# Per-tile shift of the row maxima, one two-bank output tile for a pair of score tiles, and a fourth pair turned by TensorE

## The chip, the cores and the metric

The kernel runs on one core of one Trainium2 chip. The metric is the device time of one execution in microseconds (us). Beside it stands one execution recorded by the hardware profiler; the trace's times count from that execution's first instruction.

## The reference

Three stages follow each other. Attention has a bias that a small network makes from positions; its output, with the heads side by side, passes a Fourier mixing with a two-layer network, and then a gated network.

```python
scores = scale * np.matmul(q, k.transpose(0, 1, 3, 2))      # B, H, S, D = 4, 8, 576, 64
...
scores = scores + bias.transpose(2, 0, 1)[None, :, :, :]
scores = scores - np.max(scores, axis=-1, keepdims=True)
attn = np.exp(scores)
attn = attn / (np.sum(attn, axis=-1, keepdims=True) + 1e-09)
attn_out = np.matmul(attn, v)
...
X = np.fft.fft(np.fft.fft(x, axis=1), axis=2)               # x: (4, 576, 512), heads side by side
u = x + np.real(X)
...
```

The change touches the attention stage and the way from it into the Fourier stage.

## The kernel before, in words

**Tiles.** A head pair `n` is two heads of one batch; there are 16. Each pair of head pairs gives 18 score tiles of 128 rows by 576 keys: eight of the first pair (row tiles 0 to 3, two heads), two of row tile 4 (the last 64 rows, both heads on 128 partitions, one tile for each head pair), eight of the second. They are worked two at a time: a *tile pair* `d`, 72 in all. `c = d % 9` is its place in a group of nine: places 0 to 3 are the row tiles of the first head pair, 4 the two half tiles, 5 to 8 the second head pair.

**The loop.** `attention_phase` is written for engines that run their instructions in the order of the code. One round of its loop (L572) issues work for several tile pairs, with the lags of `LAGS`:

- `scores(d)`: TensorE (PE), 12 matmuls into two PSUM tiles `sc`, of which there are three, two banks each
- `total(u)` (L413): VectorE (DVE), one custom instruction for a tile that adds the bias and takes the row maximum, which a second short instruction writes to `mm`
- `shift(d)` (L433): DVE, one TENSOR_SCALAR on two numbers a partition, minus the maxima plus a constant
- `soft(d-1)`: ScalarE (ACT), one exponential for each tile, with the shifted maximum as its bias
- turning the tile, so that keys lie on partitions. Odd `d` go by PE (`by_pe`, L445): `flip` (L475) transposes into a `sc` tile and ACT copies it to 16 bits (L484), `flip_low` (L489, DVE) makes the remainder and so frees the `sc` tile. Even `d` go by DMA: ACT copies to 16 bits (`high`), GpSimd (POOL) makes the remainder (`low`, L459), and SyncE's queue (SP) issues a DMA transpose (`turn`, L472). `FLIPS = 3` sends the last three pairs by PE whatever their number; so pair 68 is the last that the DMA turns
- `back(u)` (L493): PE, the products with `v` of the pair six rounds earlier, into a PSUM tile `po` of one bank; there are two such tiles, one for each tile of a pair
- `finish(u)` (L513): DVE, when `po` is complete (places 3, 4 and 8): row sums to factors `ri` (L523, L527), then `po` times `ri` into `x` (L531, or L541 for the half tiles). For the two tiles of a pair the steps alternate
- `store(u)` (L545): SP, `x` to a DRAM tensor `xd`

POOL also prepares the next head pair's inputs (L385 to L393).

**The end of the stage.** After round 71 the loop runs on to drain. In each round `after(d - nd)` runs `first_folds` (L779): at -3 SP loads `xd` of batch 0, at 0 the tile pool `ff` is opened on the memory of the closed pools `qk` and `sh` (which held `hl`, the source of the DMA transposes), POOL loads a sine table into it, and SP loads batches 1 and 2; at 3 batch 3. From round 1 of the drain on, two steps a round of `Folds.prep` (L728) run on DVE and ACT for batch 0. Then `fft_phase` begins on PE (L823).

**Rows of the text below.** `s` and `mm` are written by L421, `mm` by L435; `pt` is a turned tile; `lowa`, `lowb` and `raw` are large buffers (bias, inputs, later the loaded `xd`).

Of the kernel before, what the change touches and what calls it, by code (L numbers as in the profile page):

```python
# [9 lines left out]
F32 = mybir.dt.float32  # L10
# [5 lines left out]
ALU = mybir.AluOpType  # L16
PSUM = bass.MemoryType.PSUM

B, H, S, D = 4, 8, 576, 64
# [3 lines left out]
PSC = 2.0**14  # L23
PSH = 14 * math.log(2.0)
# [26 lines left out]
QW = S + 64  # L51
RAW = 2 * (S + 2 * QW)
LAGS = 1, 2, 3, 3, 3, 6
FLIPS = 3
SB = 4
PB = 4
HLB = 3
# [3 lines left out]
def pool(tc, **kw):  # L61

    return tc.tile_pool(reuse_waits="tile", **kw)
# [281 lines left out]
def attention_phase(tc, nc, io, vs, bias, biasl, raw, xd, ident, last, after, es, right):  # L345
# [7 lines left out]
    rq, st, live, pts, outs, xs, hls, mms, Ps = {}, {}, {}, {}, {}, {}, {}, {}, {}  # L353
    pairs = [(b, p) for b in range(B) for p in range(NP)]
    units = []
# [3 lines left out]
    nu = len(units)  # L359
# [53 lines left out]
    def total(u):  # L413
        n, t, h = units[u]
        sc = live.pop(u)
        bv = bias[t // 2][:, t % 2, 2 * pairs[n][1] + h] if t < 4 else biasl[:, pairs[n][1]]
        s = sp.tile([128, S], F32, tag="s", name="s", bufs=SB)
        if u % 2 == 0:
            mms[u // 2] = wp.tile([128, 2, 2], F32, tag="mm", name="mm", bufs=4)
        mm = mms[u // 2]  # L420
        nc.vector.tensor_tensor_reduce(  # L421
            out=s.rearrange("p (x e) -> p x e", x=2),
            in0=sc[:, :, 0:288],
            in1=bv.rearrange("p (x e) -> p x e", x=2),
            scale=0.125,
            scalar=-3.0e38,
            op0=ALU.add,
            op1=ALU.max,
            accum_out=mm[:, 0, u % 2 : u % 2 + 1],
        )  # L430
        live[u] = s

    def shift(d):  # L433
        mm = mms[d]
        nc.vector.tensor_scalar(out=mm[:, 1], in0=mm[:, 0], scalar1=-1.0, scalar2=PSH, op0=ALU.mult, op1=ALU.add)  # L435

    def soft(d):
        P = Pt[d % PB]
        mm = mms.pop(d)
        for x in range(2):  # L440
            s = live.pop(2 * d + x)
            nc.scalar.activation(out=P[:, x, 0:S], in_=s, func=AF.Exp, bias=mm[:, 1, x : x + 1], scale=1.0)  # L442
        Ps[d] = P

    def by_pe(d):  # L445

        return d % 2 == 1 or d >= nd - FLIPS

# [26 lines left out]
    def flip(u):  # L475
        d, x = divmod(u, 2)
        if x == 0:
            room(d)
        P = Ps[d][:, x]
        t = ps_s.tile([128, 2, 512], F32, tag="sc", name="turn").rearrange("p x e -> p (x e)")[:, 0:640]  # L480
# [12 lines left out]
    def back(u):  # L493
        n, t, h = units[u]
        vp = st[n]["v"]
        pt = pts.pop(u)
        if t in (0, 4):
            outs[n, t // 4, h] = ps_o.tile([128, 4, 128], F32, tag="po", name="po")
        po = outs[n, t // 4, h]
        for a in range(1 if t < 4 else 2):  # L500
            hh = h if t < 4 else a
            c = slice(0, 128) if t < 4 else slice(64 * a, 64 * a + 64)
            seq = []
            for j in range(5):
                seq += [(j, j, 0, 65), (j, j, 65, 64)]
            seq += [(5 + j, j, 0, 65) for j in range(5 if by_pe(u // 2) else 4)]
            for i, (x, j, f, w) in enumerate(seq):
                nc.tensor.matmul(  # L508
                    out=po[c, t % 4, 0:w], lhsT=pt[:, x, c], rhs=vp[:, j, hh, f : f + w],
                    start=(i == 0), stop=(i == len(seq) - 1),  # L510
                )

    def finish(u):  # L513
        n, t, h = units[u]
        if t < 3:
            return
        if n not in xs:
            xs[n] = xp.tile([128, 5, 128], F32, tag="x", name="x") if n + 1 < len(pairs) else last
        x = xs[n]
        po = outs.pop((n, t // 4, h))  # L520
        w = 4 if t == 3 else 1
        ri = wp.tile([128, 4], F32, tag="ri", name="ri", bufs=4)
        nc.vector.tensor_scalar(  # L523
            out=ri[:, 0:w], in0=po[:, 0:w, 64], scalar1=PSC * 1e-9, scalar2=vs[:, 0:1], op0=ALU.add, op1=ALU.mult
        )
        yield
        nc.vector.reciprocal(out=ri[:, 0:w], in_=ri[:, 0:w])  # L527
        yield
        if t < 4:
            f = 64 * h if 2 * pairs[n][1] >= H // 2 else 64 - 64 * h  # L530
            nc.vector.tensor_tensor(  # L531
                out=x[:, 0:4, f : f + 64],
                in0=po[:, :, 0:64],
                in1=ri.rearrange("p (w o) -> p w o", o=1).to_broadcast([128, 4, 64]),
                op=ALU.mult,
            )
        else:
            for a in range(2):
                f = 64 * a if 2 * pairs[n][1] >= H // 2 else 64 - 64 * a
                r = slice(64 * a, 64 * a + 64)  # L540
                nc.vector.tensor_scalar(  # L541
                    out=x[0:64, 4, f : f + 64], in0=po[r, 0, 0:64], scalar1=ri[r, 0:1], scalar2=None, op0=ALU.mult
                )

    def store(u):  # L545
        n, t, h = units[u]
        if (t, h) != ((3, 1) if n % 2 else (4, 0)) or n + 1 == len(pairs):
            return
        b, p = pairs[n]
        p = p if 2 * p >= H // 2 else H // 4 - 1 - p  # L550
        f = slice(128 * p, 128 * p + 128)
        x = xs.pop(n)
        nc.sync.dma_start(out=xd[b][0:512, f].rearrange("(t p) d -> p t d", p=128), in_=x[:, 0:4])
        nc.sync.dma_start(out=xd[b][512:S, f], in_=x[0:64, 4])

    yield [lambda n=n, nm=nm: load(n, nm) for n in range(2) for nm in "kqv"]
    yield from prep(0)
# [1 line left out]
    wp = es.enter_context(pool(tc, name="att", bufs=3))  # L559
    sp = e1.enter_context(pool(tc, name="sh", bufs=3, side="right"))  # L560
    xp = es.enter_context(pool(tc, name="xs", bufs=2))
    ps_s = es.enter_context(pool(tc, name="ps_s", bufs=3, space=PSUM))
    ps_o = es.enter_context(pool(tc, name="ps_o", bufs=2, space=PSUM))
    Pt = [wp.tile([128, 2, QW], F32, name=f"P{x}", bufs=1) for x in range(PB)]
    for P in Pt:
        nc.gpsimd.memset(P[:, :, S:QW], 0.0)
# [1 line left out]
    L1, L2, L3, L4, L6, L5 = LAGS  # L568
    nd = nu // 2
    flips = [2 * d + x for d in range(nd) if by_pe(d) for x in range(2)]  # L570
    lows = []
    for d in range(nd + L5 + 2):  # L572
        us = (2 * d, 2 * d + 1) if d < nd else ()
        bs = (2 * (d - L5), 2 * (d - L5) + 1) if 0 <= d - L5 < nd else ()
        fin = [finish(u) for u in bs]

        def step():
            for f in fin:
                next(f, None)

        c = d % 9
        n = 2 * (d // 9) + (c >= 5)
        if us and c in (0, 5) and n + 1 < len(pairs):
            nxt = prep(n + 1)

        for x in lows:
            flip_low(*x)
        lows = []
        if 0 <= d - L1 < nd:
            soft(d - L1)  # L590
        if us:
            scores(d)
        for x in range(2):
            if x == 0 or not us:
                if flips and flips[0] // 2 <= d - L6:
                    lows.append(flip(flips.pop(0)))
            if bs:
                back(bs[x])
        if 0 <= d - L2 < nd:
            high(d - L2)  # L600
        if us:
            total(us[0])
        if 0 <= d - L3 < nd:
            low(d - L3)
        if 0 <= d - L4 < nd:
            turn(d - L4)
        if us:
            next(nxt, None)
            total(us[1])
            shift(d)  # L610
        step()
        if us:
            next(nxt, None)
        step()
        step()
        if us and n + 2 < len(pairs):
            for nm in {0: "k", 1: "q", 2: "v"}.get(c - 5 * (c >= 5), ""):
                load(n + 2, nm)
        for u in (2 * (d - L5 - 1), 2 * (d - L5 - 1) + 1):
            if 0 <= u < nu:  # L620
                store(u)
        if d == nd:
            e1.close()
        after(d - nd)
# [32 lines left out]
TP = 290  # L657
T2 = 289
F_LOAD = -3
F_PREP = 1  # L660
F_STEPS = 2
F_MAX = 5
# [27 lines left out]
class Folds:  # L690
# [82 lines left out]
    def ahead(self, n):  # L773

        if self.done < n:
            next(self.flow, None)


def first_folds(folds):  # L779

    def after(n):
        if n == F_LOAD:
            folds.load(0)
        if n == 0:
            folds.open()
            for b in range(1, B - 1):
                folds.load(b)

        if n == 3:
            folds.load(B - 1)  # L790
        for _ in range(F_STEPS):
            if n >= F_PREP:
                folds.ahead(F_MAX)

    return after
# [965 lines left out]
```

## Time and profile before

| | us |
|---|---|
| median of 3 runs | 1143.27 |
| lowest, highest | 1139.97, 1145.56 |
| the profiled execution | 1141.91 |
| its span, first to last instruction | 1140.0 |

So 1.9 us of the profiled execution lie outside its span, and it is 1.4 us faster than the median. In the span PE is busy for 1030.9 us (90%), DVE 728.8 (64%), ACT 553.5 (49%), POOL 292.1 (26%). Those are means over stages that differ: up to 127 us the bias is made, attention's loop runs from there to about 370 us, its drain to 406, the Fourier stage begins at 406.7, and from about 500 us on PE works almost without a gap. A time in the trace is read as start and duration; a note in brackets is the engine's idle time just before, with the event that ended it.

### The profile page before, as it was taken

To read this page: it belongs to the slowest core of one execution; us is meant where nothing else is said; L and a number is where in the kernel's file an instruction comes from. 1 tells how busy PE (TensorE), PEld (TensorE's weight loads), DVE (VectorE), ACT (ScalarE), POOL (GpSimd) and SP (SyncE) were. 2 spreads that over 40 slices of the span, in tenths; PEclk is the share of its full clock that TensorE was granted. 3 is DMA by queue.
4 is the path that set the end of the run, shared out by engine and by line. 5 is a ranking of instruction groups with operands and counts; after the bars stand their busy time and mean duration, and the time that the engine had idled before them with its cause. 6 is when DMAs were issued, how large, how long until landed. Compare 5 with 4: busy or idle time off the path is not lost.

```text
span 1140.0 us, 25690 instructions
## 1 busy us (share of the span) xinstructions
PE 1030.9 (90%) x10711; PEld 943.3 (83%) x10711; DVE 728.8 (64%) x1826; ACT 553.5 (49%) x1047; POOL 292.1 (26%) x250
## 2 busy tenths in 40 slices
PE   6999877878878299969999999999999999999998
PEld 4778776767777178658999999999999989898997
DVE  5998899999999387477796523334495165352512
ACT  3888788888888234454452212212254234333322
POOL 2777687877676000000000000000001120101000
PEclk8999899999999699989999999999999999999999
DMA  5542177778776940014451000000133000101011
GB/s 164 175 135 89 34 162 168 162 159 168 161 175 125 140 136 1 19 56 130 120 186 48 1 1 2 1 1 1 57 111 109 1 1 1 38 1 47 1 38 47
DMA packets 116626, 90.40 MB, mean 79 GB/s; under 512 B 85721, under 2 KB 97117, under 8 KB 116253
## 3 DMA queue, kind: packets, MB, share of 16 engines
q1 hardware_dynamic: 113496, 79.88, 28.2%
q10 hardware_dynamic: 2724, 5.90, 1.6%
q0 software_dynamic: 288, 2.97, 1.2%
q8 instruction: 84, 1.38, 0.5%
q14 instruction: 34, 0.27, 0.1%
HBM read 58.95 MB, written 9.14 MB: 60 GB/s over the span
## 4 chain that ended last, share of the span: by engine, by line
PE 65%; DVE 17%; POOL 6%; issue 4%; DMA 4%; ACT 3%; SPq 0%; ACTq 0%; POOLq 0%; DVEq 0%
PE h L1287 18%; PE acc L1323 17%; PE psp L1459 5%; PE pu L1434 4%; PE po L1481 4%; POOL hl L459 3%; PE pv L1382 3%; PE y L823 3%; DMA pt<-hl 2%; PE D L870 2%; DVE pt L491 2%; DVE s L421 2%; PE bps L267 2%; DVE bt L311 2%; PE sc L408 2%
## 5 line engine op out<-in xcount | busy, mean ns | idle before, releaser
L1291 ACT ACTIVATE gh<-h 128x256 fp32r<-128x256 f32 x144 | 55.2, 383 | 249.1 <-PE h L1287 246.8
L1292 DVE SCALAR_TENSOR_TENSOR gl<-h,gh 128x256 fp32r<-128x256 f32 x144 | 60.9, 423 | 175.2 <-ACT gh L1291 174.3
L1287 PE MATMUL h<-uh,wh 128*128 128x256 f32 x576 | 162.9, 283 | 2.2 <-DVE gl L1292 2.0
L1323 PE MATMUL acc<-gh,wh 128*128 128x256 f32 x576 | 163.7, 284 | 0.0
L1287 PE MATMUL h<-uh,wl 128*128 128x256 f32 x576 | 162.0, 281 | 1.1 <-DVE wl L995 1.1
L1323 PE MATMUL acc<-gh,wl 128*128 128x256 f32 x576 | 161.7, 281 | 1.4 <-DVE wl L995 1.4
L1287 PE MATMUL h<-ul,wh 128*128 128x256 f32 x576 | 161.9, 281 | 0.0
L1323 PE MATMUL acc<-gl,wh 128*128 128x256 f32 x576 | 161.4, 280 | 0.0
L1079 POOL MEMSET w<- 64x288 f32 x2 | 0.7, 335 | 491.6 <-ACT wsq L976 491.5
L1287 PEld LDWEIGHTS h<-uh,wh 128*128 128x128 f32 x576 | 109.6, 190 | 3.1 <-DVE gl L1292 2.5
L442 ACT ACTIVATE P<-s,mm 128x576 f32<-128x576 f32 x144 | 103.2, 766 | 17.0 <-DVE mm L435 17.0
L1287 PEld LDWEIGHTS h<-uh,wl 128*128 128x128 f32 x576 | 109.6, 190 | 1.3 <-DVE wl L995 1.3
L1323 PEld LDWEIGHTS acc<-gh,wl 128*128 128x128 f32 x576 | 109.0, 189 | 1.7 <-DVE wl L995 1.6
L1287 PEld LDWEIGHTS h<-ul,wh 128*128 128x128 f32 x576 | 109.3, 190 | 0.1
L1323 PEld LDWEIGHTS acc<-gl,wh 128*128 128x128 f32 x576 | 108.9, 189 | 0.3
L1323 PEld LDWEIGHTS acc<-gh,wh 128*128 128x128 f32 x576 | 108.8, 189 | 0.4
L508 PE MATMUL po<-vp,pt 128*128 128x65 f16 (+3 forms) x2322 | 84.1, 196 | 22.3 <-DMA pt<-hl 21.4
L508 PEld LDWEIGHTS <-pt 128*128 128x128 f16 (+1 forms) x2322 | 80.7, 101 | 25.4 <-DMA pt<-hl 21.8
L482 PE MATMUL turn<-ident,P 128*128 128x128 f32 x370 | 57.0, 286 | 45.9 <-DVE pt L491 45.4
L459 POOL TENSOR_TENSOR hl<-P,hl 128x1024 f16<-128x1024 f32 x70 | 88.6, 1289 | 29.5 <-PE sc L408 13.0
L482 PEld LDWEIGHTS turn<-ident,P 128*128 128x128 f32 x370 | 40.7, 144 | 58.8 <-issue 34.3
L250 ACT ACTIVATE mask<-pre 128x576 f16<-128x576 f32 x96 | 61.1, 652 | 25.8 <-PE pre L247 24.5
(245 smaller groups left out, 2665.8 us busy)
## 6 DMA issues: line engine op xcount, KB each, us to landing
w<-in_w_ch SPq DMA_DIRECT2D x32, 512.0 KB, 3.5
vld<-in_v ACTq DMA_DIRECT2D x16, 320.0 KB, 3.5
raw<-in_q SPq DMA_DIRECT2D x16, 320.0 KB, 4.1
raw<-in_v SPq DMA_DIRECT2D x16, 320.0 KB, 4.0
raw<-in_k SPq DMA_DIRECT2D x16, 288.0 KB, 3.2
w<-in_w_in SPq DMA_DIRECT2D x8, 512.0 KB, 3.5
out<-o SPq DMA_DIRECT2D x16, 256.0 KB, 2.0
xd<-x SPq DMA_DIRECT2D x15, 256.0 KB, 4.1
```

The source lines that it names most:

```text
L250: nc.scalar.activation(out=m.rearrange("p (x e) -> p x e", x=2), in_=p[:, :, 0:288], func=AF.Sigmoid, scale=1e30)
L442: nc.scalar.activation(out=P[:, x, 0:S], in_=s, func=AF.Exp, bias=mm[:, 1, x : x + 1], scale=1.0)
L459: nc.gpsimd.tensor_tensor(out=hl[:, :, o : o + c], in0=P[:, :, j : j + c], in1=hl[:, :, j : j + c], op=ALU.subtract)
L482: nc.tensor.transpose(t[:, 128 * k : 128 * k + 128], P[:, 128 * k : 128 * k + 128], ident)
L508: nc.tensor.matmul(out=po[c, t % 4, 0:w], lhsT=pt[:, x, c], rhs=vp[:, j, hh, f : f + w], start=(i == 0), stop=(i == len(seq) - 1),)
L1287: nc.tensor.matmul(out=h, lhsT=st[:, q], rhs=mv[:, k], start=(n == 0), stop=(n == 11))
L1291: nc.scalar.activation(out=gh, in_=h, func=AF.Relu)
L1292: nc.vector.scalar_tensor_tensor(out=gl, in0=h, scalar=0.0, in1=gh.bitcast(F32), op0=ALU.max, op1=ALU.subtract)
L1323: nc.tensor.matmul(out=acc[x, d // 2][:, d % 2], lhsT=st[:, q], rhs=mv, start=(e == 0 and d % 2 == 0 and n == 0), stop=(e == NF - 1 and d ...
L1434: nc.tensor.matmul(out=p[:, 0:CH], lhsT=st[:, q], rhs=mv[:, kk, e], start=(n == 0), stop=(n == 11))
L1459: nc.tensor.matmul(out=p[:, 0:CH], lhsT=st, rhs=mv, start=(n == 0), stop=(n == len(seq) - 1))
L1481: nc.tensor.matmul(out=p, lhsT=st[:, f, c], rhs=mv, start=(n == 0), stop=(n == 11))
```

## The change

- `shift` works on one tile, one number a partition. It follows each `total`, so there are two a tile pair.
- `back` uses one `po` tile of two banks, a bank for each tile of the pair; the pool has one such tile where it had two of one bank. `finish` runs once a tile pair, on both banks together. For the half tiles it writes all 128 partitions of `x[:, 4, 0:64]` in one instruction a head pair (the last head pair still in two), and `store` sends the two halves as two DMAs in place of one.
- `FLIPS = 4`: pair 68 is turned by PE; the last pair that the DMA turns is 66.
- `X_LOAD = 0, 3, 4`: in the drain, batch 1 is loaded at round 0, batch 2 at round 3 (was 0), batch 3 at round 4 (was 3).

```diff
-FLIPS = 3
+FLIPS = 4
...
-    def shift(d):
-        mm = mms[d]
-        nc.vector.tensor_scalar(out=mm[:, 1], in0=mm[:, 0], scalar1=-1.0, scalar2=PSH, op0=ALU.mult, op1=ALU.add)
+    def shift(u):
+        mm = mms[u // 2]
+        x = slice(u % 2, u % 2 + 1)
+        nc.vector.tensor_scalar(out=mm[:, 1, x], in0=mm[:, 0, x], scalar1=-1.0, scalar2=PSH, op0=ALU.mult, op1=ALU.add)
...
-        if t in (0, 4):
-            outs[n, t // 4, h] = ps_o.tile([128, 4, 128], F32, tag="po", name="po")
-        po = outs[n, t // 4, h]
+        if t in (0, 4) and u % 2 == 0:
+            outs[u // 18, t // 4, n % 2] = ps_o.tile([128, 2, 4, 128], F32, tag="po", name="po")
+        po = outs[u // 18, t // 4, n % 2 if t < 4 else 0][:, u % 2]
...
+        ri = wp.tile([128, 2, 4], F32, tag="ri", name="ri", bufs=4)[:, :, 0:w]
         nc.vector.tensor_scalar(
-            out=ri[:, 0:w], in0=po[:, 0:w, 64], scalar1=PSC * 1e-9, scalar2=vs[:, 0:1], op0=ALU.add, op1=ALU.mult
+            out=ri, in0=po[:, :, 0:w, 64], scalar1=PSC * 1e-9, scalar2=vs[:, 0:1], op0=ALU.add, op1=ALU.mult
         )
         yield
-        nc.vector.reciprocal(out=ri[:, 0:w], in_=ri[:, 0:w])
+        nc.vector.reciprocal(out=ri, in_=ri)
         yield
-        if t < 4:
-            f = 64 * h if 2 * pairs[n][1] >= H // 2 else 64 - 64 * h
+        if c != 4:
+            n = ns[0]
+            x = xs[n][:, 0:4].rearrange("p t (h d) -> p h t d", h=2)
             nc.vector.tensor_tensor(
-                out=x[:, 0:4, f : f + 64],
-                in0=po[:, :, 0:64],
-                in1=ri.rearrange("p (w o) -> p w o", o=1).to_broadcast([128, 4, 64]),
+                out=x if ahead(n) else x[:, ::-1],
+                in0=po[:, :, :, 0:64],
+                in1=ri.rearrange("p h (w o) -> p h w o", o=1).to_broadcast([128, 2, 4, 64]),
                 op=ALU.mult,
             )
-        else:
+            return
+        for j, n in enumerate(ns):
+            x = xs[n]
+            if n + 1 < len(pairs):
+                nc.vector.tensor_scalar(
+                    out=x[:, 4, 0:64], in0=po[:, j, 0, 0:64], scalar1=ri[:, j], scalar2=None, op0=ALU.mult
+                )
+                continue
...
-        nc.sync.dma_start(out=xd[b][512:S, f], in_=x[0:64, 4])
+        for a in range(2):
+            f = 128 * p + (64 * a if ahead(n) else 64 - 64 * a)
+            nc.sync.dma_start(out=xd[b][512:S, f : f + 64], in_=x[64 * a : 64 * a + 64, 4, 0:64])
...
-    ps_o = es.enter_context(pool(tc, name="ps_o", bufs=2, space=PSUM))
+    ps_o = es.enter_context(pool(tc, name="ps_o", bufs=1, space=PSUM))
...
             total(us[0])
+            shift(us[0])
...
             total(us[1])
-            shift(d)
+            shift(us[1])
...
+X_LOAD = 0, 3, 4
...
             folds.open()
-            for b in range(1, B - 1):
-                folds.load(b)
-
-        if n == 3:
-            folds.load(B - 1)
+        if n in X_LOAD:
+            folds.load(1 + X_LOAD.index(n))
```

On DVE, a round in which a place-3 pair is finished and the round after it, in which the half tiles are, stand before the change as follows (`ISA` is the custom instruction of `total` and the one that writes its maximum).

```order
L421 ISA s,mm<-sc,lowa 128x576
L421 ISA mm 128x1
L421 ISA s,mm<-sc,lowa 128x576
L421 ISA mm 128x1
L435 TENSOR_SCALAR mm<-mm 128x2
L523 TENSOR_SCALAR ri<-po,vs 128x4 x2
L527 RECIPROCAL ri<-ri 128x4 x2
L531 TENSOR_TENSOR x<-po,ri 128x4x64 x2
L491 TENSOR_TENSOR pt<-turn,pt 128x640
```

The same round in the changed kernel:

```order
L421 ISA s,mm<-sc,lowa 128x576
L421 ISA mm 128x1
L436 TENSOR_SCALAR mm<-mm 128x1
L421 ISA s,mm<-sc,lowa 128x576
L421 ISA mm 128x1
L436 TENSOR_SCALAR mm<-mm 128x1
L530 TENSOR_SCALAR ri<-po,vs 128x8
L534 RECIPROCAL ri<-ri 128x8
L539 TENSOR_TENSOR x<-po,ri 128x2x4x64
L493 TENSOR_TENSOR pt<-turn,pt 128x640
```

One shift has moved up between the two score tiles, and the six instructions of the finish have become three.

On SP, the last transposes and the loads of `xd` (buffers `raw`, `lowb`) stand before the change as follows.

```order
L472 DMA_TRANSPOSE pt<-hl 128x18x128 x2
L553 DMA xd_76<-x 128x4x128
L554 DMA xd_76<-x 64x128
L725 DMA raw<-xd_73 128x4x512
L726 DMA raw<-xd_73 64x512
L472 DMA_TRANSPOSE pt<-hl 128x18x128
L725 DMA lowb<-xd_74 128x4x512
L726 DMA lowb<-xd_74 64x512
L725 DMA lowb<-xd_75 128x4x512
L726 DMA lowb<-xd_75 64x512
L553 DMA xd_76<-x 128x4x128
L554 DMA xd_76<-x 64x128
```

And in the changed kernel:

```order
L474 DMA_TRANSPOSE pt<-hl 128x18x128 x2
L568 DMA xd_76<-x 128x4x128
L571 DMA xd_76<-x 64x64 x2
L742 DMA raw<-xd_73 128x4x512
L743 DMA raw<-xd_73 64x512
L742 DMA lowb<-xd_74 128x4x512
L743 DMA lowb<-xd_74 64x512
L568 DMA xd_76<-x 128x4x128
L571 DMA xd_76<-x 64x64 x2
L742 DMA lowb<-xd_75 128x4x512
L743 DMA lowb<-xd_75 64x512
```

The single transpose between the loads is gone, and the load of `xd_75` (batch 2) stands behind the last store.

## Rows read from the trace of the kernel before

**Rows 1.** Page, part 2: granted TensorE clock in tenths, 40 slices of 28.5 us.

```profile
PEclk8999899999999699989999999999999999999999
```

**Rows 2.** Pairs 9-62: length, busy (count) of PE, PEld, DVE, ACT, POOL; then L435.

```profile
153.88:341.94 188.06, 150.85 (x2659) 136.32 (x2660) 173.61 (x445) 159.51 (x226) 141.04 (x103) 0.99 0.76 167
...
153.88:341.94 188.06, 33.07 (x54) 0.99 0.76 167
```

**Rows 3.** All L435: duration ns min/median/max; then the timeline around one of them.

```profile
L435 DVE TENSOR_SCALAR mm<-mm x72: 168/310/1864, 128.6 to 369.7; 128x2 f32<-128x2 f32 x72
...
252.06 2.13 POOL L459 TENSOR_TENSOR hl<-P,hl 128x1024 f16<-128x1024 f32 x1
252.25 0.08 DVE L421 DVE_READ_ACCUMULATOR2_ANT mm<- 128x1 f32 x1
252.37 1.85 DVE L435 TENSOR_SCALAR mm<-mm 128x2 f32<-128x2 f32 x1
```

**Rows 4.** VectorE's groups: name, shapes, count | busy us, mean ns | idle before, releaser.

```profile
L491 DVE TENSOR_TENSOR pt<-turn,pt 128x640 f16<-128x640 f32 x74 | 60.3, 818 | 4.7 <-ACT pt L484 3.2
...
L435 DVE TENSOR_SCALAR mm<-mm 128x2 f32<-128x2 f32 x72 | 43.2, 600 | 2.5
...
L531 DVE TENSOR_TENSOR x<-po,ri 128x256 f32<-128x256 f32 x30 | 11.2, 416 | 0.0
```

**Rows 5.** VectorE's waits, the same stretch: us in total, times, longest.

```profile
DVE s L421 <- PE sc L408: 6.3, 18, 1.4
```

**Rows 6.** Timeline, the end of the attention stage.

```profile
370.85 7.03 SPq L472 DMA_TRANSPOSE pt<-hl  x1
...
372.24 0.61 POOL L716 DMA_DIRECT2D sin<-in_c_t  x1 [1.42 <-ACT P L442]
...
377.92 0.58 SPq L725 DMA_DIRECT2D lowb<-xd  x1
...
397.77 0.94 PE L508 MATMUL po<-vp,pt 128*128 128x65 f16 x14 [21.39 <-DMA pt<-hl]
397.85 0.69 DVE L746 TENSOR_TENSOR flo<-raw,fhi 128x512 fp32r<-128x512 f32 x1 [17.30 <-DMA pt<-hl]
...
406.70 0.30 PE L823 MATMUL y<-tt,fhi 128*1 128x290 f32 x1
```

**Rows 7.** DMA issues: KB each, median us from issue to landing.

```profile
sin<-in_c_t POOLq DMA_DIRECT2D x1, 1450.0 KB, 25.1
...
pt<-hl SPq DMA_TRANSPOSE x35, 4.6
```

**Rows 8.** Timeline of a late stage; then L1390's ns min/median/max.

```profile
930.64 1.32 POOL L1403 TENSOR_TENSOR vl<-v,vh 128x512 fp32r<-128x512 f32 x1 [6.21 <-ACT vh L1402]
...
930.75 0.15 DVE L1390 TENSOR_SCALAR ve<-mv 128x1 f32<-128x1 f32 x1
...
931.18 0.80 DVE L930 TENSOR_TENSOR ve<-ve 128x1 f32<-128x1 f32 x1 [0.27 <-ACT ve L928]
...
L1390 DVE TENSOR_SCALAR ve<-mv x18: 153/154/156, 928.2 to 1085.2; 128x1 f32<-128x1 f32 x18
```

**Rows 9.** Timeline of the rounds in which places 3 and 4 are finished.

```profile
281.82 0.34 DVE L523 TENSOR_SCALAR ri<-po,vs 128x4 f32<-128x4 f32 x2
...
282.08 0.29 DVE L527 RECIPROCAL ri<-ri 128x4 f32<-128x4 f32 x2
...
283.94 0.74 PE L482 MATMUL turn<-ident,P 128*128 128x128 f32 x5 [1.61 <-DVE pt L491]
...
284.60 1.68 PE L508 MATMUL po<-vp,pt 128*64 128x65 f16 x56
...
286.32 0.22 DVE L523 TENSOR_SCALAR ri<-po,vs 128x1 f32<-128x1 f32 x1 [0.48 <-PE po L508]
...
286.65 1.18 DVE L541 TENSOR_SCALAR x<-po,ri 64x64 f32<-64x64 f32 x4
```

**Rows 10.** Last half tile's finish to last fold; columns as in rows 2.

```profile
376.05:409.25 33.20, 10.05 (x147) 8.75 (x145) 15.56 (x28) 4.86 (x8) 0.00 (x0) 0.64 1.05 166
```

More of the change, by code (lines that the diff above doesn't have):

```diff
@@ L431, in total @@
         live[u] = s
-    def shift(d):
-        mm = mms[d]
-        nc.vector.tensor_scalar(out=mm[:, 1], in0=mm[:, 0], scalar1=-1.0, scalar2=PSH, op0=ALU.mult, op1=ALU.add)
+    def shift(u):
+        mm = mms[u // 2]
+        x = slice(u % 2, u % 2 + 1)
+        nc.vector.tensor_scalar(out=mm[:, 1, x], in0=mm[:, 0, x], scalar1=-1.0, scalar2=PSH, op0=ALU.mult, op1=ALU.add)
     def soft(d):
+        assert d - PB not in Ps
         P = Pt[d % PB]
@@ L511, in back, with ahead, finish @@
                 )
-    def finish(u):
-        n, t, h = units[u]
-        if t < 3:
-            return
[L517 to L522, printed above, removed]
+    def ahead(n):
+        return 2 * pairs[n][1] >= H // 2
+    def finish(d):
+        c = d % 9
+        if c not in (3, 4, 8):
+            return
+        ns = (2 * (d // 9), 2 * (d // 9) + 1)
+        ns = ns if c == 4 else ns[c // 8 : c // 8 + 1]
+        for n in ns:
+            if n not in xs:
+                xs[n] = xp.tile([128, 5, 128], F32, tag="x", name="x") if n + 1 < len(pairs) else last
+        po = outs.pop((d // 9, int(c == 4), int(c == 8)))
+        w = 1 if c == 4 else 4
+        ri = wp.tile([128, 2, 4], F32, tag="ri", name="ri", bufs=4)[:, :, 0:w]
@@ L538, in finish, with store @@
             for a in range(2):
-                f = 64 * a if 2 * pairs[n][1] >= H // 2 else 64 - 64 * a
+                f = 64 * a if ahead(n) else 64 - 64 * a
                 r = slice(64 * a, 64 * a + 64)
                 nc.vector.tensor_scalar(
-                    out=x[0:64, 4, f : f + 64], in0=po[r, 0, 0:64], scalar1=ri[r, 0:1], scalar2=None, op0=ALU.mult
+                    out=x[0:64, 4, f : f + 64], in0=po[r, j, 0, 0:64], scalar1=ri[r, j], scalar2=None, op0=ALU.mult
                 )
-    def store(u):
-        n, t, h = units[u]
-        if (t, h) != ((3, 1) if n % 2 else (4, 0)) or n + 1 == len(pairs):
+    def store(d):
+        n = 2 * (d // 9) + (d % 9 == 8)
+        if d % 9 not in (4, 8) or n + 1 == len(pairs):
@@ L548, in store @@
             return
         b, p = pairs[n]
-        p = p if 2 * p >= H // 2 else H // 4 - 1 - p
+        p = p if ahead(n) else H // 4 - 1 - p
         f = slice(128 * p, 128 * p + 128)
@@ L574, in attention_phase @@
         bs = (2 * (d - L5), 2 * (d - L5) + 1) if 0 <= d - L5 < nd else ()
-        fin = [finish(u) for u in bs]
+        fin = finish(d - L5) if bs else iter(())
         def step():
-            for f in fin:
-                next(f, None)
+            next(fin, None)
         c = d % 9
@@ L618, in attention_phase @@
                 load(n + 2, nm)
-        for u in (2 * (d - L5 - 1), 2 * (d - L5 - 1) + 1):
-            if 0 <= u < nu:
-                store(u)
+        if 0 <= d - L5 - 1 < nd:
+            store(d - L5 - 1)
         if d == nd:
```

## The prediction

> **What bounds the kernel now.** I read the page's slices first, then the busy times of the attention loop, then single instructions of VectorE, then the end of that stage. The clock row [rows 1] shows one hole behind the start-up: slice 14, about 370 to 399 us, at 0.6. The change works just before and in it.
>
> The loop first. From the first total of pair 9 to that of pair 63 are 54 tile pairs in 188.06 us, 3.48 us each; VectorE is busy for 173.61 of them (92%), ScalarE 159.51 (85%), TensorE 150.85 (80%), GpSimd 141.04 (75%) [rows 2]. So VectorE is the bound, with ScalarE close behind. In that sum the shift has 33.07 us for 54 instructions [rows 2], 612 ns each, for two numbers a partition. What makes it long is to be seen in its spread, 168 to 1864 ns, and in one of the long ones: it starts at 252.37, while a GpSimd instruction runs from 252.06 to 254.19, and ends at 254.22 [rows 3]. A shift that starts beside a running GpSimd instruction is held until that one ends; one that starts alone takes 0.17. Over all 72 the shift is busy 43.2 us [rows 4], so 43.2 - 72 x 0.17 = 31.0 us of it is being held.
>
> Not all of that is on the path: where VectorE is quick it next waits for the scores of TensorE, 18 times in the stretch, 6.3 us [rows 5]. A held shift swallows such a wait.
>
> Now the end. The transpose of pair 68 is issued at 370.85, the sine table's load at 372.24, the next load of `xd` at 377.92; TensorE stands idle for 21.39 us until 397.77, VectorE's fold for 17.30 until 397.85, both for this transpose, and the Fourier stage begins at 406.70 [rows 6]. The usual transpose lands 4.6 us after its issue, this one after 26.9; the sine table needs 25.1 [rows 7]. VectorE waits too because its output `flo` lies where `hl` was, which the transpose still reads.
>
> **The shift, tile by tile.** It removes 72 instructions on two numbers and adds 144 on one. What does a one-number TENSOR_SCALAR cost beside GpSimd? The trace has them in a late stage: at 930.75, 0.11 us into a GpSimd instruction that runs to 931.96, one takes 0.15 us, and right behind it a TENSOR_TENSOR is held for 0.80 us, up to 931.98; all 18 of its line take 153 to 156 ns [rows 8]. So I take the hold as gone: -31.0 us. [...]
>
> The second shift is new on VectorE and stands between the two totals. The maximum is written 0.12 us before a shift can start (252.25 to 252.37, rows 3), and the shift takes 0.15. Bounds 0.08 (the short instruction that writes the maximum, rows 3) and 0.27; I take 0.20, between: 72 x 0.20 = +14.4 us. ScalarE's first exponential may start one total earlier; I count nothing for that, since VectorE is the bound.
>
> **The joint finish.** At places 3 and 8 (16 times) two TENSOR_SCALARs take 0.34 and two reciprocals 0.29 [rows 9]; one of each, at about 0.21 and 0.18, saves 0.24. The two products of 256 elements, 0.416 each [rows 4], overlap by some 0.08; one of 512 lies between 416 ns for 256 and 818 ns for 640 elements [rows 4], an estimate of 0.68, and saves 0.07. Together 0.3, so 4.8 us. At place 4 (8 times) four instructions that take 1.18 together [rows 9] become two, 0.6 less, and one of each pair of small ones goes: about 0.85, so 6.8 us. Sum -11.6 us.
>
> One PSUM tile in place of two could make TensorE wait longer for the finish. It doesn't by this order: before, the first tile of the next place had to wait for the first product, behind both TENSOR_SCALARs, both reciprocals and 0.416 us, 0.34 + 0.29 + 0.42 = 1.05; after, for 0.21 + 0.18 + 0.68 = 1.07. At place 4 the release is earlier. Here it is no cover that is used up, but the same wait. The chain through these two rounds shows what VectorE's time is worth: TensorE's flip waits 1.61 us for `pt`, which stands behind the finish on VectorE; then 1.68 us of products; then VectorE waits 0.48 for them and has 1.18 us of finish [rows 9].
>
> The stores grow by 15 DMAs on SP, 0.58 us of that queue each, as its other issues [rows 6]; behind them stand transposes. A turned tile is read three rounds after `turn` stands in the order, 10.4 us; GpSimd's remainder (2.13, rows 3) and the landing (4.6, rows 7) take 6.7 of them. So I cost it at nothing; with that cover gone, 15 x 0.58 = 8.7 us is the most.
>
> **Sum of the loop.** On VectorE -31.0 + 14.4 - 11.6 = -28.2 us. How much of it reaches the end? ScalarE's work alone is 159.51 of 188.06 us, so the stretch can't give more than 28.5 us, and the other engines' loops stand close. In the rounds that were not held VectorE already waits for scores. I take six tenths, 17 us; bounds 5 (TensorE's and ScalarE's loops take over at once) and 28.
>
> **The drain.** Pair 68 now goes by TensorE: ten more transposes (0.74 for five, rows 9), two more copies on ScalarE, two more remainders on VectorE (0.82 each, rows 4); GpSimd and SP lose a pair. All loads now stand behind the last transpose, and `flo` is free. What is late next is VectorE: from 376.05, where the finish of the last half tiles writes `x`, to the last fold at 409.25 it is busy for 15.56 us of 33.20 [rows 10], and in the changed order all six folds stand ahead of the last remainders of pair 71. So 15.56 + 2 x 0.74 = 17.0 us of VectorE lie on the path behind 376.05, up to 393.1, then the last tile's products, 0.94 us for 14 of them at the low clock [rows 6]: the Fourier stage begins at 394.0 in place of 406.7, -13 us. Ends: 2 us, if the table and the loads, still 25 us long, hold the folds or the first sine products instead; 18, if VectorE's instructions overlap more and TensorE keeps its clock. [...] Batch 2's load is later than before, but is needed only two batches on.
>
> Behind the start of the Fourier stage the order of every engine is the same, so 733 us follow as before.
>
> **Total.** 1141.9 - 17 - 13 = 1112 us for the profiled execution. It lies 1.4 below the median of the runs, so in terms of the median 1143.3 - 30 = 1113.
>
> **The rivals.**
> A, the one-number shift is held like the old one. Then 144 shifts hold for 0.43 us each, 62 in place of 31, and VectorE gets +31.0 + 14.4 - 11.6 = +34 us; by six tenths +20, with the drain's -13 it ends at 1150, slower. The point from which the gain is gone is a mean one-number shift of 0.47 us. For it: a GpSimd instruction runs for three quarters of the time [rows 2]. Against: rows 8. Chance 0.05. [...]
> B, the loop is taken over by TensorE's and ScalarE's own loops, and VectorE's relief becomes idle time: 5 us there, 13 in the drain, 1125. For it: the busy shares of 80 and 85% and the waits in rows 5. Against: the held shifts are longer than the waits that they swallow. Chance 0.15.
> C, the change does not do what it says in the drain: the sine table and batch 1 collide, and folds or sine products wait for them. 17 in the loop, 2 there, 1124. For it: the 25.1 us of the table. Against: it was then in the queue with the long transpose. Chance 0.08.
> D, both are fuller: 27 and 18, 1098. For it: nearly all of VectorE's time in the stretch is busy. Chance 0.10.
>
> **How the numbers follow.** The forecast, 1113 (its own range 1104 to 1121), has 0.62. The range reaches to C, B and most of D: 1101 to 1127, which leaves out A, the far part of D and a little on either side. What a measurement of this kernel can tell from no change is about 0.5%, 5.7 us. Faster by more: the forecast, B, C and D, less 0.03 for their ends, 0.92. A is slower for 0.04 of its 0.05. Within: 0.04.
>
> **What would show it.** In the profile of the changed kernel: the shift's longest instruction near 0.16 us, and 144 of them busy some 22 us; one product of 0.68 at the finish; VectorE's share in the loop near or below 90% with more waits for scores; pairs of 3.2 us; no wait of TensorE for a transposed tile behind the loop, and the first product of the Fourier stage some 30 us earlier. Wrong would be: shifts with a spread up to 1.8 us (A); pairs of 3.4 us with VectorE idle (B); a new wait for the table or a load at the start of the folds (C).

## The result, and the profile after

| | before | after |
|---|---|---|
| median, us | 1143.8 (4 runs) | 1116.23 (4 runs) |
| lowest to highest | 1139.97 to 1145.56 | 1115.81 to 1117.11 |
| the profiled execution, its span | 1141.91, 1140.0 | 1117.11, 1115.3 |

The changed kernel is faster, by a ratio of 0.9764 with a 95% interval of 0.9739 to 0.979. The forecast was 1113 within 1101 to 1127.

Executions of the kernel before fall into two groups, of 1127 to 1134 (9 of 31) and 1138 to 1152 us on one chip, and the ratios are made from runs within 1.5% of the fastest, so the ratio of a variant can lie nearer to one than the medians do; the median of a_vp2 below leaves out one execution of 1165 us at a granted clock of 0.84. For that reason most readings below go by the lengths of stages within a profiled execution: *loop*, from the first total of pair 0 to the first total of pair 71; *drain*, from there to the first product of the Fourier stage; *rest*, to the end of the span. These are the marks, first of the kernel before, then of the changed one (timeline: start, duration, engine, line):

```profile
127.14 0.76 DVE L421 CUSTOM_DVE_ANT_0 s<-sc,lowa 128x576 f32<-128x576 f32 x1 [1.11 <-PE sc L408]
...
368.25 0.76 DVE L421 CUSTOM_DVE_ANT_0 s<-sc,lowb 128x576 f32<-128x576 f32 x1 [0.16 <-PE sc L408]
```

```profile
126.88 0.76 DVE L421 CUSTOM_DVE_ANT_0 s<-sc,lowa 128x576 f32<-128x576 f32 x1 [1.12 <-PE sc L408]
...
356.31 0.76 DVE L421 CUSTOM_DVE_ANT_0 s<-sc,lowb 128x576 f32<-128x576 f32 x1
...
382.39 0.43 PE L837 MATMUL y<-tt,fhi 128*1 128x290 f32 x2
```

With the 406.70 of [rows 6], before has a loop of 241.11 and a drain of 38.45; after, 229.43 and 26.08. The rest is 1140.0 - 406.70 = 733.3 and 1115.3 - 382.39 = 732.9. So 11.7 us came out of the loop and 12.4 out of the drain, and the rest stayed. Before the first total the two differ by 0.3 us. In the clock by slices, the hole of 0.6 in slice 14 [rows 1] is now 0.8:

```profile
PEclk8999899999999899879999999999999999999999
```

**The shift and the finish.** All shifts of the changed kernel (ns, min/median/max), then three of VectorE's groups (count | busy us, mean ns), which answer to [rows 3, 4]:

```profile
L436 DVE TENSOR_SCALAR mm<-mm x144: 153/154/156, 127.7 to 358.0; 128x1 f32<-128x1 f32 x144
```

```profile
L493 DVE TENSOR_TENSOR pt<-turn,pt 128x640 f16<-128x640 f32 x67 | 55.0, 821 | 11.8 <-ACT pt L486 11.7
...
L539 DVE TENSOR_TENSOR x<-po,ri 128x512 f32<-128x512 f32 x14 | 9.7, 691 | 0.5
L549 DVE TENSOR_SCALAR x<-po,ri 128x64 f32<-128x64 f32 x14 | 3.3, 279 | 0.2
```

No shift is held any more: 144 of them, none over 156 ns, 22.1 us against 43.2, although 112 of them start while a GpSimd instruction runs. The joint product takes 691 ns where two took 416 each.

**The loop.** Pairs 9 to 62 of the changed kernel (columns as in [rows 2]), then three of VectorE's waits over the whole span (total, times, longest):

```profile
151.52:330.84 179.32, 154.66 (x2659) 139.95 (x2659) 150.88 (x438) 158.19 (x227) 141.08 (x102) 0.98 0.83 175
```

```profile
DVE pt L493 <- ACT pt L486: 11.7, 17, 2.2
...
DVE ri L530 <- PE po L510: 10.6, 11, 1.4
DVE s L421 <- PE sc L408: 9.6, 24, 1.1
```

VectorE is busy for 150.88 us where [rows 2] has 173.61, so 22.7 less; the stretch became only 188.06 - 179.32 = 8.7 shorter. VectorE is at 84%, ScalarE at 88%. The first wait is the one that grew most: in [rows 4] it was 3.2 us. The second was 4.2 before; the third, for scores, was 9.8 and did not grow.

**The drain.** The stretch from the finish of the last half tiles to the first Fourier product, then its surroundings in slices of 5 us (same columns), and the two kinds of DMA of [rows 7]:

```profile
364.91:382.39 17.48, 9.25 (x136) 8.57 (x136) 16.77 (x29) 5.64 (x9) 0.00 (x0) 0.71 0.85 277
```

```profile
365.00:370.00 5.00, 0.62 (x15) 0.53 (x15) 4.73 (x10) 1.91 (x3) 0.00 (x0) 0.95 1.02 380
370.00:375.00 5.00, 4.08 (x40) 3.79 (x40) 4.97 (x6) 1.07 (x3) 0.00 (x0) 0.50 1.00 305
375.00:380.00 5.00, 3.14 (x46) 3.08 (x47) 4.63 (x10) 2.66 (x4) 0.00 (x0) 0.53 0.58 171
380.00:385.00 5.00, 4.02 (x60) 3.15 (x57) 4.76 (x12) 0.57 (x2) 0.00 (x0) 1.00 0.59 194
```

```profile
sin<-in_c_t POOLq DMA_DIRECT2D x1, 1450.0 KB, 11.4
...
pt<-hl SPq DMA_TRANSPOSE x34, 4.6
```

VectorE is now busy for 16.77 of the 17.48 us; the wait for the DMA is gone, and the table lands in 11.4 us. TensorE, busy for 0.62 us between 365 and 370, is granted 0.50 and 0.53 of its clock in the two slices that follow.

### The profile page after: what moved, and what is told of

Same layout as the page of the kernel before. It is cut to its first block, busy times and chain, and to the rows that moved or that the text cites. A ratio compares the mean times of both kernels' runs of the same rounds, so it can differ in the third digit from the quotient of the medians.

```text
span 1115.3 us, 25715 instructions
## 1 busy us (share of the span) xinstructions
PE 1035.9 (93%) x10723; PEld 947.7 (85%) x10723; DVE 700.1 (63%) x1821; ACT 554.0 (50%) x1048; POOL 289.8 (26%) x248
## 4 chain that ended last, share of the span: by engine, by line
PE 59%; DVE 5%; ACT 1%; issue 1%; DVEq 0%; ACTq 0%
PE h L1301 18%; PE acc L1337 17%; PE psp L1473 5%; PE pu L1448 4%; PE po L1495 4%; PE y L837 3%; PE pv L1396 3%; PE D L884 2%; PE xs L872 1%; DVE yl L1380 1%; DVE bs L1402 0%; DVE pt L493 0%; DVE wsq L998 0%; DVE ve L944 0%; DVE v L1407 0%
## 5 line engine op out<-in xcount | busy, mean ns | idle before, releaser
L484 PE MATMUL turn<-ident,P 128*128 128x128 f32 x380 | 59.5, 289 | 34.9 <-DVE pt L493 34.5
L461 POOL TENSOR_TENSOR hl<-P,hl 128x1024 f16<-128x1024 f32 x68 | 86.2, 1289 | 20.3 <-ACT hl L455 13.5
L250 ACT ACTIVATE mask<-pre 128x576 f16<-128x576 f32 x96 | 61.0, 651 | 25.5 <-PE pre L247 24.3
```

Source lines behind the costliest of these rows:

```text
L250: nc.scalar.activation(out=m.rearrange("p (x e) -> p x e", x=2), in_=p[:, :, 0:288], func=AF.Sigmoid, scale=1e30)
L461: nc.gpsimd.tensor_tensor(out=hl[:, :, o : o + c], in0=P[:, :, j : j + c], in1=hl[:, :, j : j + c], op=ALU.subtract)
L484: nc.tensor.transpose(t[:, 128 * k : 128 * k + 128], P[:, 128 * k : 128 * k + 128], ident)
```

## The experiments

Kernels with s_ start from the kernel before, and make one part of the change or something in its place; kernels with a_ start from the changed one. Stage lengths are those of the profiled execution, in us.

| kernel | median | ratio [95%] | loop | drain | rest |
|---|---|---|---|---|---|
| before (profile of [rows 1 to 10]) | 1143.8 | 1 | 241.1 | 38.5 | 733.3 |
| s_shift | 1124.8 | 0.990 [0.985, 0.995] | 235.2 | 24.7 | 731.7 |
| s_width | 1132.3 | 0.996 [0.991, 1.002] | 234.3 | 38.0 | 733.9 |
| s_flips | 1131.2 | 0.996 [0.992, 1.001] | 243.8 | 25.9 | 734.9 |
| s_xload | 1143.7 | 1.006 [1.000, 1.011] | 241.3 | 40.9 | 733.1 |
| s_order | 1132.4 | 0.989 [0.983, 0.996] | 242.0 | 21.6 | 738.7 |
| s_finish | 1134.9 | 0.994 [0.990, 0.999] | 234.2 | 37.1 | 734.4 |
| after | 1116.2 | 0.976 [0.974, 0.979] | 229.4 | 26.1 | 732.9 |
| a_wide | 1152.2 | 1.012 [1.008, 1.017] | 261.2 | 26.2 | 736.6 |
| a_vp | 1110.9 | 0.972 [0.966, 0.978] | 223.5 | 25.8 | 736.5 |
| a_again (after once more) | 1116.3 | 0.975 [0.972, 0.978] | 229.3 | 26.1 | 731.7 |
| a_vp2 (a_vp once more) | 1113.4 | 0.972 [0.968, 0.976] | 222.7 | 25.9 | 735.4 |
| a_steps | 1114.8 | 0.974 [0.971, 0.977] | 229.3 | 20.1 | 730.1 |
| a_both | 1106.5 | 0.967 [0.964, 0.970] | 223.5 | 19.2 | 735.7 |

s_shift, s_width, s_flips and s_xload ran on one chip, where the kernel before had a median of 1143.8; s_order, s_finish, a_wide and a_vp on a second, with 1142.3; the last four of the table on a third, with 1145.0. By the ratios alone, s_width and s_flips are not told from the kernel before. The same code varies between profiles: the loop of the kernel before, which s_xload, s_order and, up to pair 68, s_flips share, from 241.1 to 243.8; the rest, leaving out a_steps and a_both, from 731.7 to 738.7; the time up to the first total from 126.5 to 131.8. Differences of 3 us in a loop, and of a few us between medians, are to be read with that in mind.

The rest's differences arise mostly within some 70 to 220 us behind its start. Two things part the profiles there: how long TensorE's clock is low, and, at the full clock, how many products it makes in the same time. First a_again and a_vp2 from 60 to 110 us behind the start of the rest, then a_again and a_vp from 160 to 210 (columns as in [rows 2]):

```profile
442.87:492.87 50.00, 39.46 (x231) 33.24 (x230) 33.70 (x79) 24.13 (x56) 0.00 (x0) 0.90 0.15 46
```

```profile
436.18:486.18 50.00, 39.51 (x216) 32.54 (x215) 31.46 (x74) 22.53 (x51) 0.00 (x0) 0.86 0.14 42
```

```profile
542.87:592.87 50.00, 50.00 (x441) 49.95 (x440) 43.24 (x85) 24.23 (x49) 0.00 (x0) 1.00 0.44 138
```

```profile
536.33:586.33 50.00, 50.00 (x427) 50.00 (x426) 45.95 (x85) 23.76 (x49) 0.00 (x0) 1.00 0.44 138
```

The second, 427 products in place of 441 while TensorE is never idle, is so in the profiles of the kernel before, s_order, a_wide and a_vp; a run of the same products there takes 64.1 to 64.2 us, and 62.2 to 63.0 in the other profiles. What sets it is open.

### The shift alone, and its width alone

s_shift makes the shift of the change in the kernel before, after each total. s_width makes the same two instructions, but both where the one stood.

```diff
-            shift(d)
+            shift(us[0])
+            shift(us[1])
```

> The kernel before with the per-tile shift alone. Theory 1 (a shift on two numbers is held by a running GpSimd instruction, one on a single number is not): 144 shifts of 0.153 to 0.156 us, 22 us busy in place of 43, and the loop shorter by 8 to 12 us, so 1132 to 1136. Theory 2 (what helps is the first exponential starting one total earlier, the width means nothing): faster too, but with shifts that spread up to 1.8 us. Rival (the joint finish carries the loop's gain): within 3 us of before.

> The kernel before with two shifts on one number each, both at the old place behind the second total; the first exponential can start no earlier than before. Theory 1: as good as the per-tile shift or a little better, since nothing stands between the totals: 1130 to 1136. Theory 2: no gain, 1142 to 1146.

The shifts of s_shift, then of s_width (ns, min/median/max):

```profile
L436 DVE TENSOR_SCALAR mm<-mm x144: 153/154/155, 129.0 to 365.0; 128x1 f32<-128x1 f32 x144
```

```profile
L436 DVE TENSOR_SCALAR mm<-mm x144: 148/152/155, 130.9 to 365.3; 128x1 f32<-128x1 f32 x144
```

The hold is gone by the width alone: s_width takes 6.8 us out of the loop, s_shift 5.9. The place between the totals brings nothing of its own that these loops show. Both are less than six tenths of what VectorE saves (31.0 - 14.4 = 16.6 by the prediction, so 10), and less than the 8 to 12 that were expected. The medians differ by more than the loops. The profile of s_shift met a shorter form of the drain:

```profile
379.15 0.94 PE L509 MATMUL po<-vp,pt 128*128 128x65 f16 x14 [7.57 <-DMA pt<-hl]
```

There the wait for the turned tile is 7.57 us, not the 21.39 of [rows 6], with the same transpose and table in flight. So the long wait is not there in each execution. The 13.8 us between the two waits are near the 15.6 that part the medians of the two groups of the kernel before (1129.5 and 1145.1); no profile was taken in its lower group, so that the two forms make the two groups is likely and not shown. None of the ten executions of s_shift is over 1131.3, where the upper group less its 5.9 would be at 1139: it seems to meet the short form as a rule.

### The finish alone

s_finish has the joint output tile, `finish` and `store` of the change and nothing else of it.

```diff
-    ps_o = es.enter_context(pool(tc, name="ps_o", bufs=2, space=PSUM))
+    ps_o = es.enter_context(pool(tc, name="ps_o", bufs=1, space=PSUM))
...
-        fin = [finish(u) for u in bs]
+        fin = finish(d - L5) if bs else iter(())
```

> The kernel before with the joint output tile, finish and split stores alone; the shift is on two numbers, pair 68 goes by DMA. The forecast's term is -11.6 us on VectorE, six tenths of it 7 us: 1134 to 1140 where the transpose is long. Rival (one output tile makes TensorE wait for the whole finish, or the 15 more DMAs hold transposes up): same or slower, 1143 to 1150.

With overlaps counted once, VectorE is busy with the finish for 25.0 us in place of 33.0, so 8.0 less where 11.6 were forecast. The loop is 6.9 shorter, which is six tenths of the forecast term and most of the measured one. A place-3 finish before ends with the product below, which stands behind the lines of 281.82 and 282.08 in [rows 9]; the other two lines are the first and the last instruction of one in the changed kernel:

```profile
282.30 0.76 DVE L531 TENSOR_TENSOR x<-po,ri 128x256 f32<-128x256 f32 x2
```

```profile
273.67 0.23 DVE L530 TENSOR_SCALAR ri<-po,vs 128x8 f32<-128x8 f32 x1
...
274.16 0.69 DVE L539 TENSOR_TENSOR x<-po,ri 128x512 f32<-128x512 f32 x1
```

From start to end that is 1.24 us before (281.82 to 283.06) and 1.18 after. The pairs of small instructions overlapped each other and the product, so at places 3 and 8 little was to be had; the gain is at place 4. The 15 further stores show no price: the median landing of a transpose is 4.6 us, as in [rows 7].

### What holds the transpose at the end

Three kernels for it. s_flips sends pair 68 by TensorE, s_xload only moves the loads, s_order keeps pair 68 on the DMA but makes GpSimd write two numbers into the transpose's source before it may issue the table's load, so that the table waits until the transpose has read.

```diff
+            if d == nd - FLIPS - 1:
+                nc.gpsimd.memset(hl[:, 0, 0:2], 0.0)
```

> The kernel before with pair 68 turned by TensorE, loads at the old rounds. Theory 1 (the 21 us stall is this pair's DMA transpose alone): TensorE's wait for a DMA-turned tile behind the loop is gone and the Fourier stage begins some 12 us earlier, 1130 to 1133. Rival (the DMA queues are full in the drain whatever is in them, and batch 1 and 2 and the sine table come late): a new wait for a load or the table, gain under 5 us.

> The kernel before with the later loads of batches 2 and 3 alone; pair 68 still goes by DMA. If batch 2's load is what made that transpose long, it lands within 15 us and the stall falls by 10 us or so, 1134. If the sine table and batch 1 (or the transpose's own packets) did, the stall stays at about 20 us: 1141 to 1146.

> The kernel before, with a two-number GpSimd write into the source tile of pair 68's DMA transpose put ahead of the sine table's load, so that the load is issued only once that transpose has landed. Nothing else is changed. If the transpose is long because the table's packets run beside it (in the kernel before both crawl, 26.9 and 25.1 us), it now lands within 5 to 8 us, the table 8 to 13 us behind it, and TensorE's wait falls from 21 us to under 5: 1126 to 1134. If it is long because of batches 0 and 1 or of its own place in SP's queue, the wait stays near 20 us: 1140 to 1150.

s_order's timeline, then its table:

```profile
373.85 5.13 SPq L473 DMA_TRANSPOSE pt<-hl  x1
...
382.57 0.70 PE L511 MATMUL po<-vp,pt 128*128 128x65 f16 x14 [2.89 <-DMA pt<-hl]
382.63 0.10 POOL L475 MEMSET hl<- 128x2 f16 x1 [8.81 <-DMA pt<-hl]
...
383.16 0.61 POOL L719 DMA_DIRECT2D sin<-in_c_t  x1 [0.43 <-DVE raw L744]
...
392.81 0.42 PE L826 MATMUL y<-tt,fhi 128*1 128x290 f32 x2
```

```profile
sin<-in_c_t POOLq DMA_DIRECT2D x1, 1450.0 KB, 9.3
```

The transpose is through 8.8 us after its issue, at 382.6, and the table, issued behind it, lands in 9.3; TensorE waits 2.89 us in place of 21.39. Apart they take 18.1 us together; in [rows 6, 7] each of the two took over 25. s_flips ends the wait in the other way: none for a tile turned by DMA over 0.2 us, the table in 11.9 us, a drain of 25.9. s_xload leaves the two side by side; TensorE waits 23.85 us, and the drain is no shorter than before (40.9). So, by one profile of each, the long wait needs the overlap of the two. The moved loads have no share in the gain: s_flips, with the old ones, has the drain of the changed kernel (26.1).

s_order has the shortest drain of the three, 21.6. VectorE keeps two remainders less there, 1.6 us, which is not all of the difference. Its time is no better than that of s_flips; the two ran on different chips, and the rest is 3.8 us longer in its profile. What sets, when the two overlap, whether the wait is 7.6 or 21 us is not settled. In a stretch of each, the kernel before and s_shift (columns as in [rows 2]), the DMA engines are full (shares of 1.14 and 1.18), and move 118 and 253 GB/s:

```profile
373.00:397.00 24.00, 3.36 (x70) 2.80 (x69) 6.39 (x16) 3.48 (x6) 0.00 (x0) 0.66 1.14 118
```

```profile
366.00:379.00 13.00, 5.26 (x101) 4.46 (x97) 7.58 (x21) 5.08 (x8) 0.61 (x1) 0.86 1.18 253
```

### The rival that the one-number shift is held

a_wide is the changed kernel with two numbers in each of its 144 shifts, the second without use.

```diff
-        x = slice(u % 2, u % 2 + 1)
+        x = u % 2
...
+    mmt = [wp.tile([128, 2, 2, 2], F32, name=f"mm{x}", bufs=1) for x in range(4)]
```

> The changed kernel with each of its 144 shifts on two numbers a partition, the second a zero that nobody reads. Theory 1 (width decides whether GpSimd holds it): shifts spread up to 1.8 us again, over 70 us busy in place of 22, and the loop 15 to 30 us longer: 1131 to 1147; this is what rival A of the prediction would have cost. Theory 2 (placement): within 2 us of the changed kernel, 1114 to 1119.

```profile
L436 DVE TENSOR_SCALAR mm<-mm x144: 168/170/1985, 131.7 to 393.8; 128x2 f32<-128x2 f32 x144
```

The same instruction at the same place, on two numbers, is held for up to 1985 ns; its mean is 478, in sum 68.9 us. The loop is 31.8 us longer than the changed kernel's for 68.9 - 22.1 = 46.8 us of VectorE, and the time 1152.2, both more than was expected and beyond the kernel before. Against that kernel the loop is 20.1 longer, the 20 of rival A, whose 1150 was thus its price. What decides here is whether the instruction has one number or two: none over 156 ns in the changed kernel, up to 1985 in this one.

### The new wait in the loop

The pairs 17, 35 and 53, place 8 of every second group, take 4.7 us from total to total in the changed kernel, and 3.77 before. Its timeline in the first of them, on GpSimd, ScalarE, VectorE and TensorE in turn:

```profile
236.99 1.88 POOL L390 TENSOR_SCALAR raw<-raw,vs 128x640 f32<-128x640 f32 x1
...
238.90 0.75 ACT L392 ACTIVATE vp<-raw 128x640 f16<-128x640 f32 x1 [1.37 <-POOL raw L390]
239.55 1.42 ACT L444 ACTIVATE P<-s,mm 128x576 f32<-128x576 f32 x2
240.87 0.68 ACT L486 ACTIVATE pt<-turn 128x640 f16<-128x640 f32 x1
...
241.59 0.82 DVE L493 TENSOR_TENSOR pt<-turn,pt 128x640 f16<-128x640 f32 x1 [2.14 <-ACT pt L486]
...
242.47 0.77 PE L484 MATMUL turn<-ident,P 128*128 128x128 f32 x5 [2.09 <-DVE pt L493]
```

The same round before (ScalarE's copy of the values, and VectorE's remainder):

```profile
243.90 0.75 ACT L392 ACTIVATE vp<-raw 128x640 f16<-128x640 f32 x1 [0.42 <-POOL raw L390]
...
246.59 0.82 DVE L491 TENSOR_TENSOR pt<-turn,pt 128x640 f16<-128x640 f32 x1 [0.47 <-ACT pt L484]
```

In the traces of both rounds ScalarE's instructions start in the order of the code (those of the changed kernel at 238.90, 239.55 and 240.87). Its copy of the next head pair's values, `vp`, has to wait until GpSimd has scaled them, and an exponential and the copy of a turned tile stand behind it. Before, held shifts made ScalarE so late that it found the values ready but for 0.42 us; now it waits 1.37, VectorE 2.14, TensorE 2.09. a_vp moves the copy, and GpSimd's remainder of it, one round later.

```diff
+        if n > 0:
+            yield
+            yield
         nc.scalar.activation(out=T["v"][:, :, :, 0:64], in_=vv, func=AF.Copy)
```

> The changed kernel with two empty steps in the input preparation, so that ScalarE's copy of v and GpSimd's remainder of it come one round later. In the changed kernel VectorE waits 2.14 us three times for a turned tile, behind ScalarE's copy of v, which waits 1.4 us for GpSimd's scaling. If this is where a part of the loop's gain went, these waits are gone and the loop is 5 to 8 us shorter: 1108 to 1112. If GpSimd itself is the bound there, the wait moves to the next instruction that needs it: 1114 to 1118.

> The changed kernel once more, beside the three variants of it on the same chip. Both theories: 1115 to 1118, loop (first total to first total of the last pair) 229.4, drain (from there to the first Fourier matmul) 26.1, the rest 733 to 737.

> The changed kernel with ScalarE's copy of the values, and GpSimd's remainder of them, one round later. If the wait of ScalarE for GpSimd's work in every second group costs the loop its 6 us: loop 223 to 224, 5 to 6 us below the changed kernel on the same chip. If the gain seen before lay in the chip and not in the edit: within 2 us of the changed kernel on this one.

a_vp's pairs 9 to 62, then its copy in the same round, and two waits over the span:

```profile
152.24:324.84 172.60, 151.52 (x2659) 137.37 (x2659) 150.82 (x438) 157.12 (x226) 141.07 (x102) 1.00 0.88 182
```

```profile
237.93 0.74 ACT L395 ACTIVATE vp<-raw 128x640 f16<-128x640 f32 x1
```

```profile
DVE pt L496 <- ACT pt L489: 5.5, 10, 0.7
...
ACT vp L395 <- POOL raw L390: 0.7, 1, 0.7
```

The loop falls from 229.4 to 223.5, and to 222.7 in the second run; the long waits are gone, VectorE's busy time is the same. So the wait cost 6 to 7 us of the loop. The medians say it less clearly: 1110.9, and in the second run 1109.4 to 1117.7 beside the 1116.3 of the changed kernel, with a rest that is 3.6 us longer than the changed kernel's in both profiles. That comes mostly from the two things told behind the table: in a_vp the lower number of products at the full clock, in a_vp2 the longer time at the low clock.

The waits of the single parts agree. VectorE's wait for ScalarE's `pt` is 11.9 us in s_shift and 16.1 in s_width, but 3.3 in s_finish and 2.6 in a_wide, where shifts are still held. The wait came with the hold's end.

### Whether VectorE sets the drain

a_steps does one fold step a round instead of two, so that the remainders of the last pairs stand ahead of the later folds; a_both has this edit and a_vp's.

```diff
-F_STEPS = 2
+F_STEPS = 1
```

> The changed kernel with one fold step a round of the drain instead of two, so that VectorE makes the last pairs' remainders ahead of the later folds. If VectorE's work is what the drain waits for, as forecast, and the order in it matters: the last remainder, at 380.6 behind some 10 us of folds and two other remainders, comes 3 to 5 us earlier, the drain is 21 to 23 and the time 1112 to 1114, if the later folds then hide beside the first Fourier products. Rival: the folds are needed at once by the Fourier stage, so what the drain gives the rest takes: drain 22, the rest 3 to 5 us longer, time 1115 to 1118. Second rival, TensorE's clock and ScalarE's copies set the drain: 26 as before.

> The changed kernel with both edits, the later copy of the values and one fold step a round. The two lie in different stages, so the gains should add: 5.5 us for the first, and 3 to 5 for the second if VectorE's order sets the drain: 1106 to 1109. If the folds are only moved into the Fourier stage: 1109 to 1112, as with the later copy alone.

The last remainder and the first Fourier product of the changed kernel come at 380.61 and 382.39, 24.3 and 26.1 us behind the mark of pair 71; of a_steps, whose mark lies at 361.06:

```profile
379.57 0.82 DVE L493 TENSOR_TENSOR pt<-turn,pt 128x640 f16<-128x640 f32 x1 [0.23 <-ACT pt L486]
...
381.12 0.43 PE L837 MATMUL y<-tt,fhi 128*1 128x290 f32 x2
```

18.5 and 20.1 us, 6 earlier each, beyond the 3 to 5 that were expected. The folds that moved are missed a little later: the first product of the next step, `D`, starts at 391.18 in the changed kernel and at 391.97 in a_steps, which is 264.3 and 260.2 us behind the first total (126.88, 131.78). So 4.1 of the 6 us stay. In the medians it is 1.5 us, 1114.8 to 1116.3, which four runs of each don't part; the profile of a_steps came to its first total 4.3 us later than that of a_again. a_both adds both gains, 9.8 us to the changed kernel on the same chip, and with 1106.5 (1106.1 to 1111.6) it is the fastest of all.

## Why the prediction was right, and what was off in it

**The hold (-31.0) and the second shift (+14.4).** Right. No shift beside GpSimd is longer than 156 ns; from one total to the next it is now 0.86 to 0.87 us in place of 0.67, so the second shift costs the 0.20 that was taken. One number was never held, in 144 instructions of each of six kernels (means of 151 to 154 ns). Two numbers were, but not beside every GpSimd instruction, as the prediction has it: in the kernel before 43 shifts start while one runs, and 7 of these are not held (0.17 to 0.19 us), 6 of them beside its TENSOR_SCALAR (L390), which held 4 others (0.55 to 0.77). Why one number is not held and two are, and what parts those 6 from those 4, no run shows.

**The joint finish (-11.6).** Mis-sized: 8.0. The single instructions came as estimated, 0.69 us for the joint product (0.68), 0.22 and 0.20 for the small ones (0.21 and 0.18). But the forecast added the lengths of the pairs in [rows 9] as if one began where the other ended; 282.08 lies before 281.82 + 0.34. At places 3 and 8 that left 2.2 us of VectorE in place of 4.8, and at place 4 5.8 in place of 6.8.

**The share of the loop (six tenths, 17 us).** This is the term that was off most: 11.7 us, four tenths of 28.2, or just under half of 24.6, the sum with 8.0 for the finish. Pairs 9 to 62 take 3.32 us each, between the 3.2 of the forecast and the 3.4 of B, and the first Fourier product comes 24.3 us earlier in place of 30. The prediction asked what VectorE waits for next, and answered with TensorE's scores ([rows 5]); what came late was ScalarE, behind a wait for GpSimd that the held shifts had covered. With that wait moved (a_vp), the loop gives 17.6. The finish alone gave six tenths of its forecast term, the shifts alone little over a third. The bounds, 5 to 28, held it.

**The drain (-13).** It was 12.4. The mechanism holds: 16.77 us of VectorE in the 17.48 behind the last half tiles, forecast 17.0 (with 0.74 for each of two further remainders, where [rows 4] have 0.82), then the products of the last tile; taking folds out of the way shortens it. TensorE did not keep its clock, as the end of 18 supposed: 0.71 was granted over these 17.48 us. What the prediction did not see is that the long wait is a matter of the execution: where it is the short one, as in s_shift, the drain is 24.7, and nothing is to be had from it. That all four executions of the kernel before in the result lie in the upper group is luck for this term. Against its lower group, near 1130, the changed kernel gains 14 us, about what the loop gives.

**The rest, and the stores.** 732.9 against 733.3, by luck so near, since the same code took 731.7 to 738.7; no price for 15 further DMAs.

**The rivals.** A has its price, 1152, in a kernel where the shift is held. Its point of 0.47 us from which the gain is gone is too high: a_wide, with a mean of 0.478, is already 10 us slower than the kernel before. B, with 5 us from the loop, came half true: other engines took part of the gain, as one removable wait, not as their own loops. C did not come: no fold waits for the table. D's 27 us of the loop were out of reach even without the new wait.

## What to carry to other kernels

When an instruction that was held is set free, follow who was late because of it: an engine behind it may have found its inputs ready only thanks to the delay, and the new wait takes part of the gain (here ScalarE's wait for the scaled values, 0.42 us before and 1.37 after, and 6 to 7 us of the loop). A step that waits for another engine's slow work should stand as late in its queue as its reader allows. Where the kernel before shows one very long wait for a transfer (21.39 us here, 7.57 in the profile of s_shift), look at several executions before it is booked as a gain.

## What was not expected of the hardware

A DMA transpose and a plain load from GpSimd's queue, side by side, took 26.9 and 25.1 us where 8.8 and 9.3 are enough one behind the other; in another execution of nearly the same program (s_shift) the pair took 13. The two of s_order add up to 18.1 us; the pairs side by side took over 25 and 13, with loads of `xd` beside them, and what slows the one is open.

One number a partition or two parted the shifts of VectorE beside GpSimd: 0.15 to 0.16 us with one, up to 1.99 with two.

TensorE, without an idle gap and at a granted clock of 1.00, made 441 products in 50 us in some executions of a stretch and 427 in others.
